# A root first on ScalarE, the last batch's gates and output tiles by halves of the sequence, and another order

## The chip, the cores and the metric

The kernel runs on one core of one Trainium2 chip. The core has five engines with their own instruction streams: TensorE (PE, matrix products into the PSUM banks), VectorE (DVE), ScalarE (ACT), GpSimd (POOL) and SyncE (SP, which here only issues DMAs). They wait for one another through semaphores. The metric is the device time of one execution in microseconds; three executions of the kernel before were timed, and one more was profiled.

## The reference

Two stages follow each other, for 4 batches, 8 heads, a sequence of 768 and heads of 64.

- Routed attention. Each query and each key is assigned to the one of 16 centroids of its head that it is most similar to: `argmax(q/|q| . c/|c|)`. A query attends only to the keys of its own cluster: `softmax(where(same cluster, q.k/8, -1e9)) @ v`.
- A gated long convolution. The attention output `x` (4 x 768 x 512) is projected, `x1, x2, x3 = split(x @ w_proj)`; `x2` is convolved along the sequence by FFT with `filter`; the output is `(x1 * irfft(rfft(x2) * rfft(filter)) * x3) @ w_out`, float32, 4 x 768 x 512.

## The kernel before, in words

Work is cut into 8 groups (`n`, two per batch: half of the heads each) of two head pairs (`pr`). Per pair and key tile `sk`, TensorE makes the scores in three banks, ScalarE takes the exponential (lines 694 and 697), TensorE multiplies by v into a PSUM pair (line 708), and VectorE adds up the row sums (lines 725 and 729). Cluster masks are rows added to the score product: the routing of group n+1 runs beside the attention of group n, ends with one-hot rows `ohT`, and small DMAs (line 497, "aug<-ohT") put them below the q and k operands `aug`. Group 0 has no attention to hide behind: its routing (`first_masks`) is the start of the kernel, together with the centroids' normalization (lines 336 to 361, with a root on ScalarE at line 342), the cosine and sine tables of the transform (`angles`, lines 364 to 409, whose `turns` on line 377 or 379 is the first step) and constants (`constants`, lines 1003 to 1070).

The convolution of batch b (`hyena`) runs beside later attention; for the last batch nothing is left beside it. It does the forward transform (line 843 and `spectrum4`), the product with the filter's spectrum (873, 877), and then, for each of four blocks `dt` of 128 channels: the gates `G` (line 903: products for x3 and x1 in two halves `ch` of the sequence, evacuated by lines 912 and 915 into `x3`), the inverse transform `I` (926), a copy of one bank (940), folds by sum and difference into `yy` (946; of the two folds the first writes the first half of the sequence), and the product with the gates into `y2` (955). Six output tiles of 128 positions then go through `W` (981): each contracts over the four blocks of `y2`. In the last batch a tile's product is split into its first three blocks and its fourth block (985 and 987), the sixth tile is made in two halves of its columns (967 to 977), and the first two tiles share one store of 512 KB (998), while tiles 2, 3, 4 are stored singly (994) and the sixth in two halves (975).

The order of all instructions on all engines is made by a planner in the file (`Plan.place`). Each operation has a cost per engine, a due time, and the operations it depends on; the planner takes, engine by engine, the ready operation with the earliest due time. `NUDGE` holds a correction to the due time for each operation, by its running number, and `ONLY` fixes the engine of some. `after=` adds a dependency that the planner alone sees: it orders, and makes no semaphore. ScalarE needs a table for its functions; `tab=` tells the planner of it, and a table is loaded by an instruction ACT_TABLE_LOAD.

In the lists of operations below, most products of the convolution and the scores have line 84, because the helper `product` records them; they are told apart by their tiles.

Of the kernel before, what the change touches and what calls it, by code (L numbers as in the profile page):

```python
# [264 lines left out]
def build(T):  # L265
# [25 lines left out]
    def bank(i):  # L291
        return T.bank[i][:]
# [71 lines left out]
    def angles(sq):  # L364
        sins = []
        MAGIC = 12582912.0
        sc = math.pi / S
        for m in range(3):
            lo = 256 * (m // 2)
            n, r = (lambda x=x, m=m, lo=lo: x()[m % 2][:, lo // 256, :384].rearrange("p (i c) -> p i c", i=2) for x in (lambda: T.tm, lambda: T.ob))  # L370
            nk, rk = ("tm", m % 2, "a", m), ("ob", m % 2, "a", m)
            kc = lambda: T.kc
            due = 1.9 + .8 * m
            V = lambda: T.nc.vector
            def turns(e, m=m, r=r):
                if e == "ACT":
                    T.nc.scalar.activation(r(), kc(), Act.Identity, scale=T.s1t[:, m:m + 1], bias=T.magic)
# [5 lines left out]
            op(("DVE", .56), lambda e, m=m, n=n, r=r: V().scalar_tensor_tensor(  # L383
                n(), kc(), T.s0t[:, m:m + 1], r(), op0=Alu.mult, op1=Alu.add), due + .2, r=["kc", "s0t", rk], w=[nk],
               lock=True)
            def mirror(e, n=n, r=r):
                if e == "ACT":
                    T.nc.scalar.activation(r(), n(), Act.Abs)
                else:
                    V().scalar_tensor_tensor(r(), n(), -1.0, n(), op0=Alu.mult, op1=Alu.max)  # L390
            op({"DVE": .56, "ACT": .55}, mirror, due + .3, r=[nk], w=[rk], lock=True)
            A_ = lambda: T.nc.scalar.activation
            sins.append(op(("ACT", .52), lambda e, m=m, n=n: A_()(cols_(T.fwm[m][:, 1]), n(), Act.Sin, scale=sc),
                           due + 6, r=[nk], w=[("fw", m, 1)], after=[sq], tab="sin"))
# [12 lines left out]
        sins.append(op(("ACT", .39), phases, 9.5, r=["kp", "half_pi"], w=["ph"], after=[sq], tab="sin"))  # L407
        return [op(("ACT", .2), lambda e: T.nc.scalar.activation(T.warm, T.half_pi, Act.Exp), 9.6, r=["half_pi"],
                   w=["warm"], after=sins, tab="exp")]
# [164 lines left out]
    def routing(n):  # L574
# [56 lines left out]
        for ch in range(2):  # L631
            op(("DVE", .6), lambda e, ch=ch, h=h: V().transpose(T.sim[:, ch], bank(h.ids[ch])[:, :384]), b0 + 1.4 + .1 * ch,
               r=[h], w=[("sim", ch, 0), ("sim", ch, 1)], free=[h])
# [183 lines left out]
    def hyena(b):  # L817
# [66 lines left out]
        for dt in range(ND):  # L884
# [13 lines left out]
            for ch in range(2):  # L898
                for off in (2 * DM, 0):
                    h = Bank()  # L900
                    due = step(.66)

                    def G(e, dt=dt, ch=ch, off=off, h=h):
                        for kt in range(ND):
                            x = T.xT[xs][:, kt, ts(ch, 384)].rearrange("p (t n) -> p t n", n=128)
                            columns(ap(h)[:, :384].rearrange("p (t n) -> p t n", n=128), T.wpj[:, kt, off + dt * 128:off + dt * 128 + 128],
                                    x[:, :, ::-1] if ch else x, kt == 0, kt == ND - 1)
                    g = op(("PE", .648), G, due, r=XT + WPJ, w=[h], alloc=h, kind="proj",
                           after=gs[-1:] + (inv[dt - 2:dt - 1] if dt > 1 else []))
                    gs.append(g)  # L910
                    if off:
                        op(EV384, lambda e, ch=ch, x3=x3, h=h: copy(e, x3()[:, ch], ap(h)[:, :384]), due + .8,
                           r=[h], w=xkeys[ch], free=[h])
                    else:
                        op(("DVE", .55), lambda e, ch=ch, x3=x3, h=h: T.nc.vector.tensor_tensor(
                            x3()[:, ch], ap(h)[:, :384], x3()[:, ch], op=Alu.mult), due + .8,
                           r=[h], w=xkeys[ch], free=[h])
# [23 lines left out]
            for s_, o_ in ((0, Alu.add), (1, Alu.subtract))[:0 if whole else 2]:  # L941
                op(("DVE", .55), lambda e, s_=s_, o_=o_, hh=hh, sd=sd, od=od: T.nc.vector.tensor_tensor(
                    sd()[:, s_].rearrange("p a b -> p (a b)"), bk(hh, 0)[:, :384], od(), op=o_), due + 1.5,
                   r=[hh] + okeys, w=skeys[s_::2], free=[hh])
            for s_, o_ in ((0, Alu.add), (1, Alu.subtract)):
                def fold(e, s_=s_, o_=o_, yy=yy, sd=sd, hh=hh, od=od, whole=whole):
                    o = yy().rearrange("p t (g q) -> p g t q", g=2)
                    if whole:
                        x = [y[:, :384].rearrange("p (g t q) -> p g t q", g=2, q=64) for y in (bk(hh, 0), od())]
                    else:  # L950
                        x = [sd()[:, :, k].rearrange("p g (t q) -> p g t q", q=64) for k in range(2)]
                    alu(e).tensor_tensor((o[:, ::-1, ::-1, ::-1] if s_ else o)[:, :, :3], x[0], x[1], op=o_)
                op(("DVE", .55) if whole else {"DVE": .55, "POOL": 1.2}, fold, due + 2, r=[hh] + okeys if whole else skeys, w=ykeys[s_::2], lock=not whole,
                   free=[hh] if whole else [])
            op(("DVE", .95) if last else {"DVE": .95, "POOL": 2.1}, lambda e, dt=dt, x3=x3, yy=yy: alu(e).tensor_tensor(  # L955
                T.y2[:, dt], yy().rearrange("p t c -> p (t c)"), x3().rearrange("p a b -> p (a b)"),
                op=Alu.mult), due + 2.5, r=ykeys + xkeys[0] + xkeys[1], w=[("y2", dt)], lock=True)
        for tt in range(3):
            ob, obk = (T_("tm", 0), [("tm", 0, 0), ("tm", 0, 1), ("tm", 0)]) if last and tt == 2 else (
                T_("ob", tt % 2), [("ob", tt % 2, 0), ("ob", tt % 2, 1), ("ob", tt % 2)])  # L960
            for e_ in range(2):
                due = step(.87)
                if last and tt == 2 and e_:
                    for x in range(2):
                        h, cols = Bank(), ts(x, DM // 2)

                        def half(e, kts, cols=cols, h=h):
                            for kt in kts:
                                columns(ap(h)[:, :DM // 2], T.y2[:, kt, ts(NT - 1, 128)], T.wout[:, kt, cols], kt == 0, kt == ND - 1)
                        op(("PE", .36), lambda e, half=half: half(e, range(3)), due, r=[("y2", dt) for dt in range(3)] + WOUT,  # L970
                           w=[h], alloc=h, kind="proj")
                        op(("PE", .12), lambda e, half=half: half(e, range(3, 4)), due, r=[("y2", 3), h], w=[h], kind="proj")
                        op({"ACT": .37, "DVE": .42}, lambda e, cols=cols, ob=ob, h=h: copy(e, ob()[:, 1, cols], ap(h)[:, :DM // 2]), due + 1,
                           r=[h], w=[("end", x)], free=[h])
                        op({"ACT": .4, "SP": .4}, lambda e, cols=cols, ob=ob: dma(e)(
                            T.out[b].rearrange("(p t) m -> p t m", t=NT)[:, NT - 1, cols], ob()[:, 1, cols]), due + 2,
# [298 lines left out]
```

## Time and profile before

| what | value |
|---|---|
| median of three executions | 375.29 us (373.97, 375.29, 375.74) |
| the profiled execution's own time | 374.39 us |
| its span, first to last instruction | 372.7 us |
| PE busy | 359.1 us (96%) |
| DVE busy | 344.9 us (93%) |
| ACT busy | 263.9 us (71%) |
| POOL busy | 116.3 us (31%) |
| granted clock of TensorE | 1.000 |

An engine is busy while it executes. The profile lists, beside each group of instructions, how long its engine had been idle just before it and what ended that idleness. The "chain that ended last" is followed back from the last instruction, at each step to what released it. A DMA is listed twice: its issue on an engine's queue, and the time from issue to landing. Lines marked PEld are loads of weights, which overlap products.

### The profile page before, as it was taken

Reading aid. Unit: us, or ns where it says so; the run is one execution under the profiler, and the core shown is the slowest. Engines: PE = TensorE matmul, PEld = TensorE weight load, DVE = VectorE, ACT = ScalarE, POOL = GpSimd, SP = SyncE. Lnnn points to the kernel's source line nnn. Section 1 sums busy time; section 2 is a strip of 40 time slices with the busy share of each in tenths; the row PEclk is TensorE's granted clock in tenths of the full one; section 3 lists DMA queues with packets and bytes.
Section 4 is the critical chain, followed back from the end, with each engine's and each line's share of the span. In section 5 each row is a group of like instructions: output and inputs, shape, how many; then the busy total and the mean of one; then the engine's idle time right before and its main releaser. Section 6 shows DMA issues by size and latency. Waiting matters only on the chain.

```text
span 372.7 us, 8638 instructions
## 1 busy us (share of the span) xinstructions
PE 359.1 (96%) x3322; PEld 207.4 (56%) x3322; DVE 344.9 (93%) x477; ACT 263.9 (71%) x497; POOL 116.3 (31%) x158
## 2 busy tenths in 40 slices
PE   7899999999999999999999999989999999999894
PEld 3556455555654565665555556657454556566571
DVE  6998999998999899999999999998997999999993
ACT  5999878788994758788769756689764759433332
POOL 5723151220113644223223136343211342033610
PEclk9999999999999999999999999999999999999999
DMA  7879469563478748678747957357655841111204
GB/s 161 206 152 187 97 151 240 121 131 107 79 169 163 113 78 161 114 162 124 170 56 143 216 161 150 74 73 98 167 57 135 187 109 13 44 45 58 108 9 169
DMA packets 90261, 46.20 MB, mean 124 GB/s; under 512 B 78232, under 2 KB 84076, under 8 KB 90220
## 3 DMA queue, kind: packets, MB, share of 16 engines
q1 hardware_dynamic: 85308, 35.59, 39.9%
q0 software_dynamic: 2752, 8.98, 17.6%
q10 hardware_dynamic: 2160, 1.08, 1.0%
q8 instruction: 26, 0.43, 0.5%
q14 instruction: 15, 0.12, 0.1%
HBM read 31.59 MB, written 7.40 MB: 105 GB/s over the span
## 4 chain that ended last, share of the span: by engine, by line
PE 66%; DVE 20%; issue 4%; DMA 4%; SPq 2%; ACT 2%; ACTq 0%; DVEq 0%
PE bank L84 29%; PE pair L708 26%; DVE acc L729 5%; PE bank L594 4%; PE bank L843 3%; DMA aug<-ohT 3%; PE bank L627 3%; DVE tm L873 2%; SPq L497 1%; DMA qkraw<-in_q_dram 1%; DVE qkP L284 1%; DVE aug L284 1%; SPq L323 1%; PE bank L742 1%; DVE xT L808 1%
## 5 line engine op out<-in xcount | busy, mean ns | idle before, releaser
L708 PE MATMUL pair<-p,vraw 128*64 128x385 f32 x768 | 142.5, 489 | 0.0
L697 ACT ACTIVATE p<-bank 128x512 f32<-128x512 f32 x192 | 109.4, 609 | 24.2 <-PE bank L84 18.1
L729 DVE TENSOR_TENSOR acc<-p,acc 128x1536 f32<-128x1536 f32 x64 | 112.8, 1763 | 4.4 <-POOL acc L725 1.5
L84 PE MATMUL bank<-aug,aug 80*64 80x512 bf16 (+3 forms) x742 | 80.6, 326 | 2.4 <-DMA aug<-ohT 0.9
L708 PEld LDWEIGHTS pair<-p,vraw 128*64 128x64 f32 x768 | 55.6, 136 | 45.4 <-issue 38.0
L84 PEld LDWEIGHTS <-aug 80*64 80x64 bf16 (+1 forms) x742 | 44.9, 109 | 39.4 <-issue 24.7
L694 ACT ACTIVATE p<-bank 128x512 f32<-128x512 f32 x96 | 58.1, 606 | 5.8 <-PE bank L84 4.3
L84 PE MATMUL bank<-xT,wpj 128*64 128x384 bf16 x512 | 48.0, 326 | 0.2 <-ACT ohT L653 0.2
L284 POOL CAST aug<-qkP 64x768 bf16<-64x768 f32 x27 | 23.5, 875 | 74.8 <-PE bank L84 33.6
L762 POOL DMA_DIRECT2D acc<-acc x30 | 24.0, 809 | 71.9 <-DMA acc<-acc 37.1
L84 PEld LDWEIGHTS <-wpj 128*64 128x64 bf16 x512 | 30.7, 110 | 15.0 <-issue 5.2
L282 ACT COPY qkP<-bank 128x512 f32<-128x512 f32 (+1 forms) x48 | 24.3, 550 | 14.5 <-PE bank L594 9.6
L84 PEld LDWEIGHTS <-y 128*64 128x64 bf16 x472 | 23.7, 110 | 14.5 <-issue 4.3
L725 POOL TENSOR_TENSOR acc<-p,p 128x512 f32<-128x512 f32 x15 | 19.1, 1277 | 37.0 <-DVE acc L725 13.9
L873 DVE TENSOR_TENSOR tm<-bank,hm 128x512 f32<-128x512 f32 x44 | 28.1, 682 | 1.7 <-PE bank L475 0.6
L877 POOL TENSOR_TENSOR y<-tm 128x512 bf16<-128x512 f32 x15 | 19.0, 1277 | 18.1 <-DVE tm L873 5.8
L84 PE MATMUL bank<-wout,y 128*64 128x512 bf16 (+1 forms) x200 | 23.3, 371 | 0.2 <-DVE y L955 0.2
L843 PE MATMUL bank<-wpj,xT 128*64 128x512 bf16 x192 | 22.5, 379 | 0.0
L725 DVE TENSOR_TENSOR acc<-p,p 128x512 f32<-128x512 f32 x33 | 21.8, 692 | 0.1
L594 PEld LDWEIGHTS bank<-ident,qkraw 128*128 128x128 f32 x144 | 15.6, 141 | 6.2 <-issue 3.3
L594 PE MATMUL bank<-ident,qkraw 128*128 128x128 f32 x144 | 18.4, 277 | 0.1
L282 ACT CAST aug<-qkP 64x768 bf16<-64x768 f32 x21 | 17.2, 828 | 1.0 <-DVE qkP L284 0.7
(179 smaller groups left out, 432.7 us busy)
## 6 DMA issues: line engine op xcount, KB each, us to landing
vraw<-in_v_dram SPq DMA_DIRECT2D x16, 384.0 KB, 4.3
qkraw<-in_k_dram SPq DMA_DIRECT2D x30, 192.0 KB, 3.3
rb<-dr SPq DMA_DIRECT2D x30, 192.0 KB, 3.7
qkraw<-in_q_dram SPq DMA_DIRECT2D x29, 192.0 KB, 4.2
out_dram<-ob SPq DMA_DIRECT2D x10, 512.0 KB, 3.9
acc<-acc POOLq DMA_DIRECT2D x10, 384.0 KB, 5.5
acc<-acc POOLq DMA_DIRECT2D x10, 192.0 KB, 4.2
y<-in_moe_filter_fft_dram SPq DMA_DIRECT2D x4, 384.0 KB, 6.2
```

What stands on the lines that cost most here:

```text
L84: T.nc.tensor.matmul(out[64 * i:64 * i + 64], lhsT[:, 64 * i:64 * i + 64], rhs, start=start, stop=stop)
L282: T.nc.scalar.copy(out, in_)
L284: (T.nc.vector if e == "DVE" else T.nc.gpsimd).tensor_copy(out, in_)
L594: T.nc.tensor.transpose(bank(h.ids[i // 4])[:, ts(i % 4, 128)], raw(ss[i // NT], i % NT), T.ident[:, ::-1] if 3 <= i < NT else T.ident)
L694: T.nc.scalar.activation(o, ap(h).rearrange("p (a b) -> p a b", a=2), Act.Exp, scale=0.125)
L697: T.nc.scalar.activation(flat(s)[:, lo:lo + 512], ap(h), Act.Exp, scale=0.125)
L708: T.nc.tensor.matmul(o[64 * hp:64 * hp + 64, ch, :385], T.vraw[vs][:, hp, sk * D:(sk + 1) * D], T.p[slots[sk]][:, hp, 384 * ch:384 * ch + ...
L725: alu(e).tensor_tensor(o, x, y, op=Alu.add)
L729: T.nc.vector.tensor_tensor(T.acc[os], T.p[slots[sk]][:, :, :S], T.acc[os], op=Alu.add)
L762: op(("POOL", .8), lambda e, rows=rows: T.nc.gpsimd.dma_start(flat_()[:rows], flat_()[rows:2 * rows], accum_op=Alu.add), te, r=[], w=AK, b ...
L843: T.nc.tensor.matmul(ap(h)[64 * i:64 * i + 64], T.xT[xs][:, kt, c:c + 64], T.wpj[:, kt, DM:2 * DM], start=kt == 0, stop=kt == ND - 1)
L873: op(("DVE", .68), lambda e, i=i, cs=cs, r=r, h=h: T.nc.vector.tensor_tensor(T.tm[r][:, cs], ap(h), hmrow(i, (0, 2, 2, 3)[2 * r + cs]), op ...
```

## The change

- **Root first.** The memset of `half_pi` is now the first of the constants, and the activation `warm` (a square root of that constant, which loads the table with the root) is kept in a list `root`. `turns` and the zeroing copies `zero` get `after=root`, so the planner places no ScalarE computation ahead of it. The plan's cost of `turns` on ScalarE becomes 0.7 instead of 0.55, that of `tri` 2.0 instead of 1.6, and that of the routing's transposes 0.57 instead of 0.6.
- **Halves.** In the last batch the gates get a due time of their own (all first halves ahead of the second halves), and they no longer wait in the plan for the gate before them and the inverse transform two blocks earlier. The product into `y2` is made in two halves of the sequence, and an output tile depends only on the half that it lies in. The first three tiles are one product over all four blocks; the fourth and fifth, and the halves of the sixth, are still split.
- **Single stores.** The first two tiles of the last batch are stored singly, like the others.
- **Order.** All corrections `NUDGE` (1,941 before, 1,943 now) and the list `ONLY` are other ones.

```diff
-NUDGE = {0:-134.893,1:-852.116,2:-3.912,3:-64.112,4:-7.409, ...
-ONLY = {14:"POOL",15:"POOL",17:"POOL",18:"POOL",29:"ACT", ...
+NUDGE = {0:-244.575,1:-2716.133,2:-17.613,3:-10.463,4:-13.793,5:-22.114, ...
+ONLY = {13:"POOL",14:"POOL",15:"POOL",16:"POOL",18:"POOL",30:"ACT", ...
...
-            op({"DVE": .36, "ACT": .55, "POOL": .95}, turns, due, r=["kc", "s1t", "magic"], w=[rk], lock=True)
+            op({"DVE": .36, "ACT": .7, "POOL": .95}, turns, due, r=["kc", "s1t", "magic"], w=[rk], lock=True, after=root)
...
                 for off in (2 * DM, 0):
                     h = Bank()
                     due = step(.66)
+                    if last:
+                        due = w1 - 8 + 5 * ch + dt
...
                     g = op(("PE", .648), G, due, r=XT + WPJ, w=[h], alloc=h, kind="proj",
-                           after=gs[-1:] + (inv[dt - 2:dt - 1] if dt > 1 else []))
+                           after=[] if last else gs[-1:] + (inv[dt - 2:dt - 1] if dt > 1 else []))
...
-            op(("DVE", .95) if last else {"DVE": .95, "POOL": 2.1}, lambda e, dt=dt, x3=x3, yy=yy: alu(e).tensor_tensor(
-                T.y2[:, dt], yy().rearrange("p t c -> p (t c)"), x3().rearrange("p a b -> p (a b)"),
-                op=Alu.mult), due + 2.5, r=ykeys + xkeys[0] + xkeys[1], w=[("y2", dt)], lock=True)
+            for ch in range(2) if last else [slice(0, 2)]:
+                cols = slice(384 * ch, 384 * ch + 384) if last else slice(0, S)
+                op(("DVE", .55) if last else {"DVE": .95, "POOL": 2.1}, lambda e, dt=dt, ch=ch, cols=cols, x3=x3, yy=yy: alu(e).tensor_tensor(
+                    T.y2[:, dt, cols], yy().rearrange("p t c -> p (t c)")[:, cols],
+                    x3()[:, ch] if last else x3().rearrange("p a b -> p (a b)"), op=Alu.mult), due + 2.5,
+                   r=ykeys[ch::2] + xkeys[ch] if last else ykeys + xkeys[0] + xkeys[1],
+                   w=[("y2", dt, ch)] if last else [("y2", dt, 0), ("y2", dt, 1)], lock=True)
+        Y2 = lambda tile, dts: [("y2", dt, tile // 3) for dt in dts]
...
-                if last:
-                    op(("PE", .647), lambda e, W=W: W(e, range(3)), due, r=[("y2", dt) for dt in range(3)] + WOUT,
+                if last and 2 * tt + e_ > 2:
+                    op(("PE", .647), lambda e, W=W: W(e, range(3)), due, r=Y2(2 * tt + e_, range(3)) + WOUT,
                        w=[h], alloc=h, kind="proj")
-                    op(("PE", .217), lambda e, W=W: W(e, range(3, 4)), due, r=[("y2", 3), h], w=[h], kind="proj")
+                    op(("PE", .217), lambda e, W=W: W(e, range(3, 4)), due, r=Y2(2 * tt + e_, [3]) + [h], w=[h], kind="proj")
                 else:
-                    op(("PE", .862), W, due, r=[("y2", dt) for dt in range(ND)] + WOUT, w=[h], alloc=h,
+                    op(("PE", .862), W, due, r=Y2(2 * tt + e_, range(ND)) + WOUT, w=[h], alloc=h,
                        kind="proj")
...
-                if last and tt and not (tt == 2 and e_):
+                if last and not (tt == 2 and e_):
                     op({"SP": .4, "ACT": .4}, lambda e, tt=tt, e_=e_, ob=ob: dma(e)(
                         T.out[b].rearrange("(p t) m -> p t m", t=NT)[:, 2 * tt + e_], ob()[:, e_]), due + 2,
                        r=[obk[e_]], byts=157e3)
-            if not (last and tt):
+            if not last:
                 op(("SP", .4), lambda e, tt=tt, ob=ob: T.nc.sync.dma_start(
...
+    root = []
+
     def constants():
         G = lambda: T.nc.gpsimd
+        op(("POOL", .1), lambda e: G().memset(T.half_pi, math.pi / 2), -1, w=["half_pi"])
...
-        op(("POOL", .1), lambda e: G().memset(T.half_pi, math.pi / 2), -1, w=["half_pi"])
-        op(("ACT", .2), lambda e: T.nc.scalar.activation(T.warm, T.half_pi, Act.Sqrt), -1, r=["half_pi"], w=["warm"], tab="sqrt")
+        root.append(op(("ACT", .2), lambda e: T.nc.scalar.activation(T.warm, T.half_pi, Act.Sqrt), -1, r=["half_pi"], w=["warm"], tab="sqrt"))
...
-                op({"POOL": .8, "ACT": .83}, zero, 3 + (1, 1, 28)[i] * i, r=["ident"], w=[("zero", i, j)], lock=True)
+                op({"POOL": .8, "ACT": .83}, zero, 3 + (1, 1, 28)[i] * i, r=["ident"], w=[("zero", i, j)], lock=True, after=root)
```

More of the change, by code (lines that the diff above doesn't have):

```diff
@@ L43 @@
-ONLY = {14:"POOL",15:"POOL",17:"POOL",18:"POOL",29:"ACT",32:"SP",33:"SP",36:"SP",37:"ACT",39:"SP",40:"SP",41:"DVE",47:"ACT",67:"POOL",71:"ACT",85:"ACT",86:"DVE",88:"DVE",89:"DVE",91:"DVE",94:"ACT",97:"DVE",99:"ACT",100:"DVE",101:"POOL",139:"ACT",141:"DVE",143:"ACT",147:"DVE",149:"DVE",159:"ACT",176:"POOL",226:"POOL",227:"POOL",232:"POOL",233:"ACT",239:"POOL",244:"POOL",245:"DVE",253:"DVE",254:"DVE",256:"ACT",257:"ACT",357:"POOL",359:"POOL",394:"ACT",405:"DVE",407:"POOL",408:"ACT",409:"POOL",410:"ACT",412:"DVE",413:"DVE",415:"ACT",418:"DVE",426:"ACT",461:"DVE",462:"POOL",463:"DVE",498:"DVE",508:"ACT",513:"ACT",523:"POOL",533:"POOL",541:"DVE",551:"DVE",555:"ACT",559:"DVE",562:"DVE",570:"ACT",600:"DVE",608:"POOL",616:"ACT",640:"DVE",688:"ACT",690:"ACT",691:"ACT",692:"DVE",693:"DVE",694:"ACT",697:"ACT",700:"DVE",701:"POOL",702:"POOL",808:"DVE",809:"DVE",860:"POOL",861:"POOL",862:"POOL",867:"POOL",913:"POOL",914:"POOL",986:"DVE",1024:"DVE",1054:"ACT",1067:"ACT",1070:"ACT",1072:"ACT",1094:"DVE",1145:"POOL",1147:"POOL",1153:"POOL",1155:"POOL",1164:"DVE",1165:"ACT",1168:"DVE",1313:"POOL",1314:"POOL",1315:"DVE",1368:"DVE",1416:"DVE",1500:"DVE",1515:"POOL",1547:"DVE",1549:"POOL",1600:"ACT",1601:"ACT",1607:"POOL",1608:"POOL",1621:"DVE",1767:"DVE",1874:"DVE",1940:"SP"}
@@ new lines @@
+ONLY = {13:"POOL",14:"POOL",15:"POOL",16:"POOL",18:"POOL",30:"ACT",32:"SP",33:"SP",36:"SP",37:"SP",40:"ACT",41:"DVE",66:"ACT",69:"DVE",72:"POOL",73:"ACT",85:"DVE",86:"DVE",93:"DVE",94:"POOL",97:"DVE",99:"DVE",100:"DVE",101:"POOL",141:"DVE",153:"DVE",213:"ACT",226:"POOL",227:"POOL",233:"POOL",238:"POOL",244:"POOL",245:"DVE",253:"DVE",254:"ACT",257:"DVE",288:"DVE",357:"POOL",358:"DVE",359:"POOL",394:"ACT",404:"ACT",406:"DVE",407:"DVE",408:"POOL",409:"ACT",416:"POOL",417:"POOL",418:"POOL",427:"DVE",430:"ACT",461:"POOL",462:"DVE",463:"DVE",498:"DVE",525:"POOL",533:"POOL",549:"DVE",551:"ACT",555:"ACT",566:"DVE",589:"DVE",593:"POOL",594:"POOL",600:"DVE",604:"DVE",639:"DVE",691:"POOL",692:"ACT",693:"POOL",694:"POOL",696:"ACT",697:"ACT",698:"ACT",699:"POOL",700:"POOL",701:"DVE",711:"DVE",808:"POOL",809:"POOL",856:"DVE",858:"ACT",859:"ACT",861:"POOL",862:"POOL",867:"POOL",913:"DVE",915:"POOL",1002:"DVE",1005:"DVE",1018:"DVE",1067:"ACT",1070:"DVE",1072:"ACT",1075:"ACT",1077:"DVE",1146:"POOL",1147:"POOL",1152:"DVE",1153:"DVE",1154:"POOL",1156:"ACT",1164:"ACT",1168:"ACT",1201:"DVE",1313:"DVE",1315:"ACT",1369:"DVE",1416:"ACT",1421:"ACT",1426:"ACT",1448:"DVE",1457:"DVE",1516:"POOL",1600:"POOL",1601:"POOL",1607:"POOL",1608:"POOL",1609:"POOL",1610:"DVE",1621:"DVE",1812:"ACT",1875:"DVE",1886:"DVE",1919:"ACT",1920:"SP",1922:"DVE",1923:"SP",1926:"SP",1930:"SP",1933:"ACT",1934:"SP",1938:"SP",1942:"SP"}
@@ L631, in routing @@
         for ch in range(2):
-            op(("DVE", .6), lambda e, ch=ch, h=h: V().transpose(T.sim[:, ch], bank(h.ids[ch])[:, :384]), b0 + 1.4 + .1 * ch,
+            op(("DVE", .57), lambda e, ch=ch, h=h: V().transpose(T.sim[:, ch], bank(h.ids[ch])[:, :384]), b0 + 1.4 + .1 * ch,
                r=[h], w=[("sim", ch, 0), ("sim", ch, 1)], free=[h])
@@ L969, in half @@
                                 columns(ap(h)[:, :DM // 2], T.y2[:, kt, ts(NT - 1, 128)], T.wout[:, kt, cols], kt == 0, kt == ND - 1)
-                        op(("PE", .36), lambda e, half=half: half(e, range(3)), due, r=[("y2", dt) for dt in range(3)] + WOUT,
+                        op(("PE", .36), lambda e, half=half: half(e, range(3)), due, r=Y2(2 * tt + e_, range(3)) + WOUT,
                            w=[h], alloc=h, kind="proj")
-                        op(("PE", .12), lambda e, half=half: half(e, range(3, 4)), due, r=[("y2", 3), h], w=[h], kind="proj")
+                        op(("PE", .12), lambda e, half=half: half(e, range(3, 4)), due, r=Y2(2 * tt + e_, [3]) + [h], w=[h], kind="proj")
                         op({"ACT": .37, "DVE": .42}, lambda e, cols=cols, ob=ob, h=h: copy(e, ob()[:, 1, cols], ap(h)[:, :DM // 2]), due + 1,
@@ L1044, in tri @@
             G().tensor_tensor(T.tri[:].rearrange("p (b c) -> p b c", c=NC), x, T.ident[:].rearrange("p (b c) -> p b c", c=NC), op=Alu.subtract)
-        op(("POOL", 1.6), tri, 14, r=["ident"], w=["tri", ("rb", 0), ("rb", 1)])
+        op(("POOL", 2.0), tri, 14, r=["ident"], w=["tri", ("rb", 0), ("rb", 1)])
         def first_(e):
```

2 lines of the change are left out of this document (1 added, 1 removed).

## The prediction

> **What bounds the kernel now.** I read the page's table of engines first, then the busy time by stages, then the chain that ended last at both ends of the span. The rows of the stages give, for each engine, the busy time within the stretch:
>
> ```profile
> span 372.7 us, 8638 instructions
> PE 359.1 (96%) x3322; PEld 207.4 (56%) x3322; DVE 344.9 (93%) x477; ACT 263.9 (71%) x497; POOL 116.3 (31%) x158
> ...
> 10.00:25.00 15.00, 13.32 (x126) 8.34 (x126) 14.06 (x33) 14.38 (x30) 8.83 (x19) 1.00 0.89 191
> 25.00:330.00 305.00, 302.38 (x2739) 171.70 (x2738) 288.27 (x365) 229.67 (x433) 88.84 (x93) 1.00 0.63 126
> 330.00:367.50 37.50, 36.08 (x437) 23.74 (x435) 35.05 (x63) 13.62 (x27) 12.94 (x10) 1.00 0.13 51
> ```
>
> From 25 to 330 us PE is busy for 302.38 of 305.00 us: the body is TensorE's, and no order can take more than 2.62 us out of it. From 10 to 25 the full engines are ACT (14.38 of 15) and DVE (14.06), and PE stands still for 1.68. From 330 to 367.5 PE (36.08 of 37.5) and DVE (35.05) share the bound, and ACT has two thirds of the time free. After 367.5 only copies and stores are left. So the change can win at the two ends, and its new order can win little and lose much between them.
>
> **The start.** ScalarE's own sequence, in order of time:
>
> ```profile
> 1.82 1.28 ACT L377 ACT_TABLE_LOAD   x1 [1.82 <-DVE s1t L1029]
> 3.12 1.30 ACT L377 ACTIVATE ob<-x,magic,s1t 128x384 f32<-128x384 f32 x2
> 4.33 0.83 ACT L1060 ACTIVATE aug<-ident 64x768 bf16<-64x768 f32 x1
> ...
> 7.12 0.84 ACT L1060 ACTIVATE aug<-ident 64x768 bf16<-64x768 f32 x1 [1.97 <-DMA qkraw<-in_q_dram]
> 7.98 1.28 ACT L342 ACT_TABLE_LOAD   x1
> ...
> 9.28 0.20 ACT L342 ACTIVATE s<-ss 128x1 f32<-128x1 f32 x1
> 9.39 0.84 ACT L282 COPY qkP<-bank 128x384 f32<-128x384 f32 x2
> ...
> 10.34 1.28 ACT L393 ACT_TABLE_LOAD   x1
> ...
> 18.99 1.28 ACT L408 ACT_TABLE_LOAD   x1
> ```
>
> There are four table loads in the span: these two, one ahead of the sines at 10.34 and one ahead of the first exponential at 18.99. The first load serves `turns`, which isn't a root; after the root's load at 7.98 a copy runs at 9.39 with no further load. With the root first, its table serves turns, zeros and copies, and the load at 7.98 goes: -1.28 us of ACT. The other two stay.
>
> Is it on the path? VectorE's rows say how much:
>
> ```profile
> 8.12 0.15 DVE L341 TENSOR_SCALAR ss<-ss 128x1 f32<-128x1 f32 x1
> 8.20 0.61 DVE L383 SCALAR_TENSOR_TENSOR tm<-x,s0t,ob 128x384 f32<-128x384 f32 x1
> 8.84 0.56 DVE L390 SCALAR_TENSOR_TENSOR ob<-tm 128x384 f32<-128x384 f32 x1
> ```
>
> The root's input is there at 8.27, so the root could run 1.0 us earlier; but DVE fills that second with lines 383 and 390, work that must be done anyway. Hence only the relief of ACT counts, in a stretch where both ACT and DVE are full and several copies can go to either. `ONLY` also pins five of the six zeros to POOL where it pinned four, which takes one more zero (0.84 us, the row at 7.12) from ACT. POOL pays 0.74 us for it, and has 6.2 us free between 10 and 25:
>
> ```profile
> L1058 POOL MEMSET aug<- 64x768 bf16 x4 | 2.9, 744 | 3.1 <-DVE ob L390 3.0
> ```
>
> Together ACT loses 1.28 + 0.84 = 2.1 us; spread over two full engines that is about 1.0 us. Since the loads of q and k end part of the waits, I take **-0.7 us**. Ends: -1.68 (all of PE's standstill) and +0.2: the root itself, 0.20 us, now stands between the first load and `turns`, whose result DVE needs.
>
> The moved memset takes 0.10 us on POOL; by its due time it passes the iotas and the identity on POOL's queue, which feed `s1t` and DVE's first turn. I cost it at nothing: its cover is the 1.82 us that ACT stands idle ahead of its first load. Without that cover it is 0.10. On ACT's queue the root passes two turns, two zeros and a copy pair; those wait for 0.20 us more. The other changed planner costs move no work by themselves.
>
> **The end.** First the chain that ended last, then TensorE's list and the copies and issues behind it:
>
> ```profile
> 361.94 0.56 DVE qkP L915
> 362.50 0.46 DVE sim L952
> 362.96 0.46 DVE qkP L915
> 363.42 0.47 DVE sim L952
> ...
> 363.92 0.97 DVE y L955
> ```
>
> ```profile
> 352.56 1.43 PE L84 MATMUL bank<-inv,y 128*64 128x192 bf16 x30 [1.12 <-DVE y L877]
> ...
> 361.66 3.08 PE L84 MATMUL bank<-wout,y 128*64 128x512 bf16 x30
> 364.93 2.46 PE L84 MATMUL bank<-wout,y 128*64 128x256 bf16 x26 [0.19 <-DVE y L955]
> ```
>
> ```profile
> 367.22 0.37 ACT L282 COPY tm<-bank 128x256 f32<-128x256 f32 x1
> ...
> 367.44 0.69 DVE L284 COPY ob<-bank 128x512 f32<-128x512 f32 x1 [0.61 <-PE bank L84]
> ...
> 367.63 0.36 ACTq L975 DMA_DIRECT2D out_dram<-tm  x1
> 368.16 0.47 ACTq L994 DMA_DIRECT2D out_dram<-ob  x1
> ```
>
> ```profile
> L994 ACTq DMA_DIRECT2D out_dram<-ob x2: 374/420/466, 366.2 to 368.2; - x2
> ...
> DMA to landing us min/median/max: 3.2/3.2/3.2
> ```
>
> ```profile
> L975 ACTq DMA_DIRECT2D out_dram<-tm x1: 362/362/362, 367.6 to 367.6; - x1
> ...
> DMA to landing us min/median/max: 3.0/3.0/3.0
> ```
>
> Call T the end of the last product into `y2`, 363.92 + 0.96 = 364.88. All six tiles wait for it. Behind it: 26 products, 2.46 us, to 367.41; a copy to 368.13; an issue at 368.16, landed 3.2 us later, at 371.4 (the row of line 994); and 1.3 us to the end of the span.
>
> After the change only tiles 3 and 4 and both halves of tile 5 need T, each for its fourth block. The 26 products are 16 wide and 10 half-wide ones, 21 wide equivalents at 0.117 us; 4 wide and 4 half-wide are left behind T, 6 equivalents, **0.70 us** instead of 2.46. Last then is a half tile: copy 0.37, issue 0.03 later, landing in 3.0 (what the half tile's store on line 975 took), and the same 1.3: T + 0.05 + 0.70 + 0.02 + 0.37 + 0.03 + 3.0 + 1.34 = T + 5.5, where it was T + 7.8. The single stores of tiles 0 and 1 are one issue more and come earlier, beside other work; if not, an issue costs 0.36 to 0.47 us (the rows above).
>
> But T moves. The 1.76 us of products go ahead of T, where PE's only idle time from 351 on is 1.12 + 0.19 = 1.31 us. The gates, freed from the gate and the inverse ahead of them, are what could fill the 1.12 (`xT`, which they read, is written long before, and in this batch each block has its own `x3`), so T is pushed by at least 0.45. VectorE pays too: `y2` in halves costs two operations less their overlap. The chain's row pairs a 128x384 operation of 0.56 with a next one that adds 0.46, so a pair is 1.02 against 0.95; four pairs, +0.28. T later by 0.45 + 0.28 = 0.73 us gives an end at T(before) + 6.2, **-1.6 us**. Ends: -2.3 (T unmoved) and +0.6 (nothing earlier, and no overlap in the halves: 2 x 0.56 - 0.97 = 0.15, four times).
>
> [...]
>
> **The body.** All corrections of the order are new, and the diff doesn't tell where each instruction lands. The rows nearest to it are the three waits of PE around one handover of masks from one group to the next:
>
> ```profile
> 242.88 0.84 PE L84 MATMUL bank<-xT,wpj 128*64 128x384 bf16 x8 [0.21 <-ACT ohT L653]
> ...
> 248.90 0.52 PE L84 MATMUL bank<-aug,aug 128*64 128x256 bf16 x4 [0.94 <-DMA aug<-ohT]
> ...
> 249.89 0.90 PE L84 MATMUL bank<-aug,aug 80*64 80x512 bf16 x6 [0.47 <-ACT p L694]
> ```
>
> Together they are 1.62 us of the body's 2.62. I take **0**: the same products by the same engine. Ends: -2.6 (none of it left) and +4.9 (three more handovers of the seven like this one).
>
> **Sum.** -0.7 - 1.6 + 0 = -2.3 us. Against the profiled execution's 374.39 that is 372.1; that execution lies 0.9 under the median of the three timed. I put the sum to the mean of all four, 374.85: **372.6 us**. A difference of 0.5%, 1.9 us, is about what this kernel's measurement can tell from none.
>
> **Rivals.**
>
> *The end stays as it is* (374.1). The last stores are bound by bandwidth, not by T:
>
> ```profile
> 366.80:367.80 1.00, 0.60 (x8) 0.12 (x4) 0.39 (x2) 0.79 (x2) 0.00 (x0) 1.00 0.80 299
> ...
> 369.80:370.80 1.00, 0.00 (x0) 0.00 (x0) 0.00 (x0) 0.00 (x0) 0.00 (x0) 1.00 1.01 370
> ```
>
> For these four slices the DMA share is 0.8 to 1.07 at 299 to 406 GB/s, which moves the last batch's 1.57 MB. If PE, full until T, finishes tiles 0 to 2 only just before T, their stores still queue with the others, and the end gains nothing: -0.7 alone, 374.1. Against it: the first half's last product into `y2` needs only the fold at 362.50, and at its 0.56 us could end near 363.9.
>
> *Slower: late masks in the body* (377.4). The new order puts the mask chain of more groups too late, and PE, which has no slack there, waits at each handover for the DMA "aug<-ohT", then for an exponential, as at 248.90. Price 1.62 each. Two eat the gain (2.3 / 1.62 = 1.4); from three on the kernel is slower by over 0.5%: 374.85 - 2.3 + 4.9 = 377.4. For it: PE is at 99% there, so any slip shows. Against it: before, one handover in seven did so.
>
> *The body gains too* (370.0): -2.3 - 2.6. Against it: every wait would have to go, though the new order was free to move them.
>
> *The first computation isn't the root's or its load isn't saved*: -1.6 alone, 373.2, still inside the forecast's own spread.
>
> **How the numbers follow.** Forecast with its spread (371.7 to 374.1: for the start -1.2 to -0.25 and for the end -1.95 to -0.5, half way to the bounds of each): 0.50, of which 0.10 within 0.5% of no change. End unchanged: 0.16, nearly all within. Late masks: 0.26, of which 0.03 within. Body gains: 0.08, faster. That makes faster 0.40 + 0.08 + 0.02 = 0.50, same 0.10 + 0.14 + 0.03 = 0.27, slower 0.23. The range reaches from 370.0, the case in which the body gains, to 378.0, past three late handovers; about one in ten lies beyond each end.
>
> **What would show it.** Three table loads, the first ahead of line 1050's activation, and none at the centroids' root; the first exponential 0.7 us earlier. At the end: products into `y2` as eight 128x384 ones of 0.55; at most 0.8 us of tile products behind the last of them; stores starting more than 1.5 us ahead of the last; 5.5 us from T to the end of the span. In the body: PE's idle time between 25 and 330 us near 2.6. The prediction is wrong if that idle time is above 5, if T comes more than 1.5 us later against the end of attention, or if PE waits for the first group's routing longer than before.

## The result, and the profile after

The changed kernel takes **370.86 us** (370.64 to 371.05, four executions), the kernel before 375.48 (373.97 to 375.74): a ratio of 0.9885, with a 95% interval of 0.9858 to 0.9912. The forecast was 372.6. The profiled executions differ by less: 370.64 against 374.39, spans 368.9 against 372.7, so 3.8 us of the 4.6 can be looked for in the traces.

First the head of the page of the changed kernel and its busy time by stages (columns as in the prediction: stretch, its length, then busy time and instructions of PE, PEld, DVE, ACT, POOL, the granted clock, the DMA share, GB/s):

```profile
span 368.9 us, 8653 instructions
PE 357.5 (97%) x3314; PEld 208.9 (57%) x3316; DVE 342.5 (93%) x478; ACT 263.6 (71%) x495; POOL 120.9 (33%) x162
10.00:25.00 15.00, 13.92 (x128) 7.79 (x130) 14.20 (x28) 13.74 (x29) 9.17 (x28) 1.00 0.88 190
25.00:330.00 305.00, 302.55 (x2745) 175.41 (x2745) 287.85 (x367) 230.11 (x431) 91.59 (x93) 1.00 0.61 126
330.00:364.70 34.70, 33.55 (x412) 21.68 (x408) 32.45 (x62) 12.37 (x25) 12.96 (x10) 1.00 0.17 65
```

PE stands idle for 2.45 us of the body, against 2.62. So the body is still TensorE's, and the gain is at the ends. Five moments make that exact: the first and the last product of attention (line 708), T (the end of the last product into `y2`), the first store's issue, and the end of the span.

| us | first product | last product ends | T | first store | end |
|---|---|---|---|---|---|
| before | 26.48 | 325.90 | 364.88 | 365.68 | 372.7 |
| after | 24.77 | 322.58 | 362.43 | 361.83 | 368.9 |

The start is 1.71 shorter, attention 299.42 → 297.81 (-1.61), and what follows it 46.8 → 46.3 (-0.5). The middle one is mostly no gain. The busy time of the instructions that read or write `xT`, the operand of the projection, says where it went. Each fence has two rows, attention and what follows it; the columns are the stretch, its length, PE, PEld, DVE, the granted clock, the DMA share and GB/s. First before, then after:

```profile
25.00:325.90 300.90, 49.70 (x492) 8.50 (x144) 14.63 (x14) 1.00 0.63 127
325.90:367.40 41.50, 20.25 (x216) 2.75 (x48) 2.24 (x3) 1.00 0.15 55
```

```profile
25.00:322.58 297.58, 48.19 (x470) 8.76 (x144) 14.09 (x14) 1.00 0.63 128
322.58:364.63 42.05, 21.67 (x232) 2.90 (x48) 2.15 (x3) 1.00 0.17 63
```

Sixteen gate products, 1.42 us of PE, have moved behind the last product of attention. For equal work, that is with these 1.42 us counted where they were, the body is 0.2 shorter and the end 1.9.

ScalarE and VectorE in the start of the changed kernel, in order of time:

```profile
1.27 1.31 ACTq L323 DMA_DIRECT2D qkraw<-in_k_dram  x2
2.62 1.28 ACT L1059 ACT_TABLE_LOAD   x1 [2.62 <-issue]
3.92 0.20 ACT L1059 ACTIVATE warm<-half_pi 128x1 f32<-128x1 f32 x1
...
5.36 0.51 ACT L388 ACTIVATE ob<-tm 128x384 f32<-128x384 f32 x1
5.77 0.19 ACT L342 ACTIVATE s<-ss 128x1 f32<-128x1 f32 x1
...
6.46 0.51 ACT L388 ACTIVATE ob<-tm 128x384 f32<-128x384 f32 x1
6.99 1.28 ACT L395 ACT_TABLE_LOAD   x1
...
21.02 1.28 ACT L408 ACT_TABLE_LOAD   x1
...
22.93 0.60 ACT L697 ACTIVATE p<-bank 128x512 f32<-128x512 f32 x1 [0.41 <-PE bank L84]
```

```profile
8.22 1.02 DVE L284 COPY qkP<-bank 128x384 f32<-128x384 f32 x2
...
14.06 0.55 DVE L529 TENSOR_REDUCE mx<-bank 128x24 f32<-128x384 f32 x1
```

The last of these rows, in the kernel before:

```profile
16.61 0.56 DVE L529 TENSOR_REDUCE mx<-bank 128x24 f32<-128x384 f32 x1
```

There are three table loads of 1.28 us, and the centroids' root at 5.77 has none ahead of it: between the loads at 2.62 and 6.99 ScalarE runs the root of the constant, turns, a zero, mirrors and the centroids' root. Two mirrors of the angles (`Abs`, line 388) run on ScalarE where VectorE had all three (line 390), ScalarE issues two loads ahead of its table, and the one-hot steps (line 529) begin at 14.06, where they began at 16.61.

The end of the changed kernel: TensorE, then VectorE, then SyncE.

```profile
357.87 0.28 PE L84 MATMUL bank<-wout,y 128*64 128x256 bf16 x2
359.22 5.41 PE L84 MATMUL bank<-wout,y 128*64 128x256 bf16 x54 [1.07 <-DVE y L959]
```

```profile
354.88 1.02 DVE L959 TENSOR_TENSOR y<-yy,qkP 128x384 bf16<-128x384 f32 x2
...
361.88 0.55 DVE L959 TENSOR_TENSOR y<-sim,qkP 128x384 bf16<-128x384 f32 x1
...
364.67 0.69 DVE L284 COPY ob<-bank 128x512 f32<-128x512 f32 x1 [1.90 <-PE bank L84]
```

```profile
361.83 0.33 SPq L982 DMA_DIRECT2D out_dram<-tm  x1
...
363.55 2.17 SPq L1001 DMA_DIRECT2D out_dram<-ob  x4
```

And the first store before:

```profile
365.68 0.33 SPq L975 DMA_DIRECT2D out_dram<-tm  x1
```

The tile products run without a gap from 359.22 to 364.63, 2.2 us beyond T (361.88 + 0.55 = 362.43). The last is a whole tile of the **first** half of the sequence (512 wide, copied at 364.67); the tiles of the second half went ahead.

### The profile page after: what moved, and what is told of

It reads as the page before. It is cut to its first block, busy times and chain, and to the rows that moved or that the text cites. A ratio compares the mean times of both kernels' runs of the same rounds, so it can differ in the third digit from the quotient of the medians.

```text
span 368.9 us, 8653 instructions
## 1 busy us (share of the span) xinstructions
PE 357.5 (97%) x3314; PEld 208.9 (57%) x3316; DVE 342.5 (93%) x478; ACT 263.6 (71%) x495; POOL 120.9 (33%) x162
## 4 chain that ended last, share of the span: by engine, by line
PE 78%; DVE 11%; ACT 5%; issue 3%; DMA 1%; POOL 1%; SPq 0%; DVEq 0%; ACTq 0%; POOLq 0%
PE bank L84 33%; PE pair L708 28%; PE bank L843 5%; PE bank L594 5%; DVE acc L729 3%; PE bank L627 2%; ACT p L697 1%; PE bank L82 1%; DMA qkraw<-in_k_dram 1%; DVE qkP L284 1%; PE bank L475 1%; PE bank L742 1%; ACT p L694 1%; PE bank L607 1%; DVE ohT L655 1%
## 5 line engine op out<-in xcount | busy, mean ns | idle before, releaser
L84 PE MATMUL bank<-aug,aug 80*64 80x512 bf16 (+3 forms) x736 | 81.9, 327 | 2.1 <-ACT p L697 0.9
L708 PEld LDWEIGHTS pair<-p,vraw 128*64 128x64 f32 x768 | 56.6, 136 | 43.8 <-issue 36.7
L284 POOL CAST aug<-qkP 64x768 bf16<-64x768 f32 x29 | 25.9, 900 | 83.3 <-DVE acc L729 55.9
L84 PE MATMUL bank<-xT,wpj 128*64 128x384 bf16 x504 | 47.2, 326 | 0.0
L282 ACT COPY qkP<-bank 128x512 f32<-128x512 f32 (+1 forms) x46 | 23.1, 559 | 15.9 <-PE bank L594 9.7
L282 ACT CAST aug<-qkP 64x768 bf16<-64x768 f32 x28 | 23.2, 830 | 1.0 <-DVE qkP L284 0.4
L877 POOL TENSOR_TENSOR y<-tm 128x512 bf16<-128x512 f32 x14 | 17.8, 1277 | 12.8 <-DVE tm L873 10.6
L732 ACT COPY osb<-pair 128x770 f32<-128x770 f32 x16 | 12.9, 806 | 10.8 <-PE pair L708 10.7
```

Of the source, the lines that this page charges most:

```text
L84: T.nc.tensor.matmul(out[64 * i:64 * i + 64], lhsT[:, 64 * i:64 * i + 64], rhs, start=start, stop=stop)
L282: T.nc.scalar.copy(out, in_)
L284: (T.nc.vector if e == "DVE" else T.nc.gpsimd).tensor_copy(out, in_)
L708: T.nc.tensor.matmul(o[64 * hp:64 * hp + 64, ch, :385], T.vraw[vs][:, hp, sk * D:(sk + 1) * D], T.p[slots[sk]][:, hp, 384 * ch:384 * ch + ...
```

## The experiments

The two theories at the outset: **P**, the parts (root first, halves, single stores) bring the gain; **O**, the new order brings it, whatever the parts. The gates' own due times, and their freedom from the gate and the inverse transform ahead of them, count as order here: e2, e3 and e4 keep them, e6 and e7 don't have them. All moments are those of the table above, idle time is PE's between 25 us and the last product of attention. Ratios are to the kernel before, run beside them on the same chip.

| run | first product | last product | T | first store | end | idle | ratio [95%] |
|---|---|---|---|---|---|---|---|
| before | 26.48 | 325.90 | 364.88 | 365.68 | 372.7 | 2.62 | |
| after | 24.77 | 322.58 | 362.43 | 361.83 | 368.9 | 2.45 | 0.9885 [0.9858, 0.9912] |
| e1 after, root late | 25.63 | 323.35 | 363.19 | 362.59 | 369.7 | 2.30 | 0.9920 [0.9893, 0.9947] |
| e2 after, whole products | 25.08 | 322.90 | 363.19 | 364.30 | 371.1 | 2.21 | 0.9949 [0.9913, 0.9985] |
| e3 after, paired store | 24.88 | 322.63 | 362.48 | 361.87 | 369.4 | 2.29 | 0.9890 [0.9840, 0.9941] |
| e4 order alone | 25.64 | 324.83 | 365.13 | 366.24 | 373.4 | 3.73 | 0.9971 [0.9935, 1.0007] |
| e5 before, root first | 26.20 | 325.86 | 364.84 | 365.63 | 372.6 | 2.86 | 0.9956 [0.9919, 0.9993] |
| e6 before, halves | 26.51 | 327.33 | 366.85 | 366.80 | 374.2 | 4.16 | 0.9989 [0.9954, 1.0025] |
| e7 before, all parts | 26.18 | 328.29 | 367.79 | 367.74 | 375.1 | 4.53 | 0.9979 [0.9949, 1.0010] |
| e8 after, copies spread | 25.07 | 322.71 | 362.55 | 361.95 | 369.0 | 2.19 | 0.9875 [0.9832, 0.9919] |
| e9 before, root and mirrors | 26.24 | 325.51 | 364.16 | 364.95 | 371.9 | 2.32 | 0.9973 [0.9938, 1.0008] |
| e10 after, mirrors on DVE | 25.60 | 322.96 | 362.82 | 362.21 | 369.3 | 2.17 | 0.9898 [0.9857, 0.9938] |
| e11 after, casts on DVE | 26.87 | 324.55 | 364.39 | 363.78 | 370.9 | 2.38 | 0.9924 [0.9894, 0.9953] |
| e12 e9 and one load earlier | 25.36 | 325.79 | 364.41 | 365.20 | 372.2 | 3.63 | 0.9934 [0.9898, 0.9969] |

### Parts taken out of the changed kernel

In the edits, `move(n, m)` puts operation n right behind m in the finished order, or first where m is None.

**e1**, the root behind the centroids' root again:

```diff
     order = P.place(...)
+    move(10, 25)    # 10: warm; 25: the centroids' root
```

> The changed kernel with its own order, but the root of the constant moved on ScalarE from first place to behind the centroids' root; nothing else moves. Theory P (the parts bring the gain: at the start the saved table load): a load of 1.28 us returns ahead of the centroids' root, the first product with v comes 1.0 to 1.3 us later than in the changed kernel (24.77 us), and the time is 371.9 to 372.1 us. Theory O (the new order brings it, whatever the parts): the first product with v comes at most 0.3 us later, 370.9 to 371.1 us.

The first product comes 0.86 later, less than the 1.0 to 1.3 expected, and the end of the span 0.8; the median is 372.17 us. In this order the root is worth 0.86 of its load's 1.28 us, and ScalarE has four table loads again.

**e2**, the product into `y2` whole, and all tiles split 3 + 1 as before; every other operation keeps its correction of the due time:

```diff
-            for ch in range(2) if last else [slice(0, 2)]:
...
+            op(("DVE", .95) if last else {"DVE": .95, "POOL": 2.1}, lambda e, dt=dt, x3=x3, yy=yy: alu(e).tensor_tensor(
+                T.y2[:, dt], yy().rearrange("p t c -> p (t c)"), x3().rearrange("p a b -> p (a b)"), op=Alu.mult), due + 2.5,
+               r=ykeys + xkeys[0] + xkeys[1], w=[("y2", dt, 0), ("y2", dt, 1)], lock=True)
...
-                if last and 2 * tt + e_ > 2:
+                if last:
```

> The changed kernel, but in the last batch the product with the gates into y2 in one piece per block, and tiles 0 to 2 split in three blocks and one as before; the order is the same up to these operations, and the planner places them anew. Theory P: every tile waits for the last product into y2, the time from its end to the end of the span grows from 6.5 us to 7.5 or more, and the time is 371.9 to 372.5 us. Theory O (TensorE has no time free ahead of that product, so it only changes which tiles come first): within 0.4 us of the changed kernel, 370.5 to 371.3 us.

373.47 us, 2.6 above the changed kernel and above the range expected by P; the spans differ by 2.2. From the last product of attention to the end it is 48.2 us, 1.9 more than 46.3. TensorE's list shows the price, a gap:

```profile
358.18 0.38 PE L84 MATMUL bank<-wout,y 128*64 128x512 bf16 x2
361.12 1.92 PE L84 MATMUL bank<-wout,y 128*64 128x512 bf16 x16 [2.56 <-DVE y L961]
363.24 3.44 PE L84 MATMUL bank<-wout,y 128*64 128x512 bf16 x38 [0.20 <-DVE y L961]
```

**e3**, tiles 0 and 1 in one store of 512 KB again:

```diff
-                if last and not (tt == 2 and e_):
+                if last and tt and not (tt == 2 and e_):
...
-            if not last:
+            if not (last and tt):
```

> The changed kernel, but tiles 0 and 1 of the last batch in one store of 512 KB. Theory P: the pair waits for the later of the two copies and moves twice the bytes at the end, 0.2 to 0.5 us more, 371.1 to 371.4 us. Theory O: no difference above 0.2 us.

371.2 us, and 0.5 more of span. One slice of the last transfers shows why; the slices beside it have 0.97 and more:

```profile
364.40:365.40 1.00, 0.27 (x4) 0.00 (x0) 0.69 (x1) 0.14 (x1) 0.00 (x0) 1.00 1.02 382
365.40:366.40 1.00, 0.00 (x0) 0.00 (x0) 0.00 (x1) 0.00 (x0) 0.00 (x0) 1.00 0.55 213
366.40:367.40 1.00, 0.00 (x0) 0.00 (x0) 0.00 (x0) 0.00 (x0) 0.00 (x0) 1.00 0.97 401
```

The store waits for the second of its tiles (the copy ends at 365.40, the issue is at 365.46), and the DMA engines run half empty meanwhile (0.55).

**e4**, the three edits together, so that of the change only the order is left:

> The changed kernel's order with all three parts undone (root late, products into y2 whole, pair store). Theory P: the sum of the three losses, 1.1 + 1.3 + 0.3, 373.3 to 374.0 us, so that the order alone gives about 2 us of the 4.6. Theory O: at most 1 us of loss, 370.9 to 371.9 us.

374.18 us, a ratio whose interval reaches 1. The order alone gives 0.84 of the start. From the last product to the end it is 48.6 us against 46.8; 1.42 of that are the moved gates, and the gap of e2 stands in it, so that for equal work the end is 0.4 longer. The 1.9 of e2 and the 0.5 of e3 make up the 2.3 by which this end is longer than the changed kernel's 46.3. Theory O falls in its simple form.

### Parts put into the kernel before

**e5** (first edit), **e6** (second edit: the product into `y2`, its dependents and the stores as in the change's diff; the first three tiles stay split 3 + 1) and **e7** (both), in the old order:

```diff
     order = P.place(...)
+    move(9, None)    # half_pi's memset
+    move(10, 30)     # warm, behind ScalarE's first load of q
```

```diff
+            for ch in range(2) if last else [slice(0, 2)]:
...
-                if last and tt and not (tt == 2 and e_):
+                if last and not (tt == 2 and e_):
```

> The kernel before with its own order; only the memset of the constant moves to the front of GpSimd's queue and the root of it to the front of ScalarE's computations. Theory P: one table load fewer, the first product with v 0.4 to 0.7 us earlier than at 26.48 us, 374.6 to 375.0 us. Theory O: the load goes, but VectorE has other work in that second, so the first product with v moves by less than 0.3 us, 375.2 to 375.6 us.

> The kernel before with its own order up to the last batch's products into y2; these are made in halves, each output tile depends on its half, and tiles 0 and 1 are stored singly; the gates keep their order. Theory P: the end gains 1.0 to 1.6 us, 373.9 to 374.5 us. Theory O (PE is full until the last product into y2, so nothing can be taken ahead of it): at most 0.4 us, 375.1 to 375.5 us.

> Both of the former: the kernel before with its own order, the root first, the halves and the single stores. Theory P: the sum of the two, 373.2 to 373.8 us. Theory O: 374.9 to 375.5 us.

The root alone moves the first product by 0.28 us (ratio 0.9956); the halves alone give 376.71 us, a ratio of 0.9989; all parts 0.9979. From the last product to the end it is 46.9 in e6 and 46.8 in e7, where it was 46.8. So P falls too: **in the old order the parts bring nothing that can be told (0.9979), in the new one 0.9% or 3.3 us (e4 to after, 0.9971 to 0.9885, 374.18 to 370.86 us)**. Each needs the other. For the halves the reason is in e2 and e6: the new order puts nearly all tile products behind the gates, where whole products into `y2` leave PE waiting for 2.56 and 0.20 us, and halves cut that to the one wait of 1.07 in the list of the changed kernel. The old order has no such gap to fill: in the prediction's rows PE waits there for 1.12 and 0.19, in e6 for 1.1 and 0.5.

**e8** swaps two of the last copies between VectorE and ScalarE in the changed kernel, to have the last copy on the free engine:

```diff
+ONLY.update({1929: "DVE", 1922: "ACT"})
```

The expectation counts the tiles from one: operation 1929 copies tile 3 in the numbering from zero that is used above, and 1922 copies tile 1, the last one.

> The changed kernel with the last copies of output tiles spread differently: the copy of tile 4 moves from ScalarE to VectorE, which stands idle there for 1.9 us, and the last one, of tile 2, from VectorE to ScalarE. The last copy is then 0.59 instead of 0.69 us and the stores ahead of it leave up to 0.5 us earlier: 0.1 to 0.4 us less, 370.4 to 370.8 us. If the end is set by the last tile's product alone, 0.1 us less at most.

371.96 us (370.81 to 373.38), span 369.0: no difference that can be told. The stores of this run:

```profile
361.95 0.33 SPq L983 DMA_DIRECT2D out_dram<-tm  x1
...
363.67 2.06 SPq L1002 DMA_DIRECT2D out_dram<-ob  x4
```

Counted from the first store, the last issue ends at 3.78 us instead of 3.89, as was meant, but the span ends at 7.1 in both. Three slices of the changed kernel fit that, with the DMA engines full (0.98 to 1.02):

```profile
363.90:364.90 1.00, 0.73 (x8) 0.14 (x4) 0.23 (x1) 0.60 (x2) 0.00 (x0) 1.00 0.98 352
364.90:365.90 1.00, 0.00 (x0) 0.00 (x0) 0.46 (x1) 0.00 (x0) 0.00 (x0) 1.00 1.02 383
365.90:366.90 1.00, 0.00 (x0) 0.00 (x0) 0.00 (x0) 0.00 (x0) 0.00 (x0) 1.00 0.98 385
```

So within this 0.1 us the last tile doesn't set the end. That the stores' volume does, counted from the first issue, is argued from the full engines.

### What else shortens the start

The root's 0.86 leaves half of the 1.71 open.

**e9**, in the kernel before, root first and two mirrors on ScalarE; **e10**, the changed kernel with these back on VectorE; **e11**, the changed kernel with three casts on VectorE:

```diff
+    move(9, None)
+    move(10, 30)
+    for n in (44, 56):
+        find(n).on = "ACT"
```

```diff
+    for o in order:
+        if o.seq in (44, 56):
+            o.on = "DVE"
```

For e11 the last has (66, 73, 95) in place of (44, 56).

> The kernel before with the root first, as in the run with the root alone, and two of the three mirrors of the first features (the operation of line 390) on ScalarE, where the changed order has them. Theory V (VectorE's queue up to its last one-hot step sets the start, so what is taken off it comes back): 2 x 0.56 us leave VectorE, ScalarE does them in 2 x 0.51, and the first product of attention comes about 1.0 us earlier than with the root alone, near 25.2 us; the body may take some of it back. Theory S (the start is set by ScalarE or by the loads): first product of attention within 0.3 us of the 26.2 us with the root alone, or later.

> The changed kernel with the same two mirrors back on VectorE, 2 x 0.56 us there, and 2 x 0.51 off ScalarE; nothing else moves. Theory V: first product of attention 0.9 to 1.1 us later than the 24.77 of the changed kernel, and the time later by about as much. Theory S: first product of attention and time within 0.3 us of the changed kernel's, since VectorE stands idle somewhere in that stretch.

> The changed kernel with three casts into aug (64x768), which its order gives to ScalarE (0.83 us each), back on VectorE (0.55 us each), where the kernel before has them. Theory V: up to 3 x 0.55 = 1.65 us more on VectorE ahead of the last one-hot step, so the first product of attention comes 1.0 to 1.7 us later than 24.77. Theory S: ScalarE gets 2.5 us free, and the first product of attention comes no later than in the changed kernel.

In the changed order VectorE's queue does set the start: e10 has the first product 0.83 later (0.9 to 1.1 were expected), e11 2.10 later (1.0 to 1.7 were expected), although ScalarE is busy for 0.9 and 4.2 us less between 10 and 25. Of e10's 0.83 only 0.4 is left at the end of the span. In the old order e9 gives nothing: 26.24 against 26.20. Its rows on TensorE and VectorE say why:

```profile
9.90 0.55 PE L607 MATMUL bank<-ident,qkraw 128*128 128x128 f32 x3 [2.33 <-DMA qkraw<-in_q_dram]
```

```profile
10.48 1.95 DVE L284 COPY qkP<-bank 128x384 f32<-128x384 f32 x4 [0.93 <-PE bank L607]
```

Most of the second that came free is spent waiting for transposes, and they wait until 9.90 for a load of q that ScalarE issues late.

**e12** adds that load early, behind ScalarE's first one (the changed order has it early too, on SyncE at 1.84):

```diff
+    move(37, 30)     # a half of q, 6.45 before
```

> The kernel before with the root first and two mirrors on ScalarE, as in the run before, and one more thing of the changed order: the load of a half of q that ScalarE issued at 6.45 us is issued behind its first load of q, near 1.9, ahead of the activations. In the run without this, VectorE stood idle for 0.93 us until 10.48, behind transposes that waited until 9.90 for that load. Theory V with loads (the relief of VectorE counts once the loads come early enough): transposes near 7.5, that idle time gone, and the first product of attention up to 0.9 us earlier than the 26.24 without it, 25.3 to 25.8. Theory B (the DMA engines are full in that stretch, so an earlier load makes another one late): the first product of attention within 0.3 us of 26.24, and the wait stands at another load.

25.36, 0.88 earlier than e9: the wait was the cover. (373.54 us, ratio 0.9934.) The load without the mirrors wasn't run; in e5 VectorE comes to these copies at 10.45 without a wait, so there was none for an earlier load to remove. The body gave the start back in this execution, by a wait of PE's:

```profile
65.04 1.51 PE L594 MATMUL bank<-ident,qkraw 128*128 128x128 f32 x12 [1.64 <-DMA qkraw<-in_q_dram]
```

### DMA waits in the body

That wait isn't e12's own. In the lists of PE's waits between 25 us and the end of attention, all six profiled kernels with the old order wait for the DMA "aug<-ohT", 0.5 to 1.0 us, and four of them (e5, e6, e7, e12) for a load into `qkraw` or `vraw` besides, 0.7 to 1.7. Of the eight with the new order none waits for a DMA there; e4's idle time of 3.73 has a wait of 1.4 for a row sum in it instead. The times fit in part: on one chip the kernel before took 373.66 to 378.45 us in 25 executions, e3 370.98 to 371.56 in 4, and e1 371.38 to 373.46 in 10; but e2 took 372.55 to 375.06 and e4 373.89 to 376.76 in 10 each, without such a wait in their profiles. Each kernel has one profile, so that these waits make the spread is argued and not shown.

The granted clock of TensorE is a second candidate. Of those 25 executions the six with a clock of 0.993 or less took 376.51 to 378.45 us, the eleven with 0.998 or more 373.66 to 377.87: it goes with a part of the spread and leaves most of it. It doesn't carry the verdict on the old order: by the medians of the executions at 0.997 or more alone, e4, e6 and e7 stand at 0.9986, 1.0002 and 1.0003 of the kernel before.

## Why the prediction was right, and where it wasn't

Faster, as forecast, and by more: -4.6 us instead of -2.3 (from the run's own medians), -3.8 in the traces. The 370.86 us lie inside the range, but below the forecast's own spread (371.7 to 374.1) and next to the 370.0 of the rival in which the body gains too. The traces show no such gain, so that closeness is chance.

**The start: mechanism half right, size wrong.** The saved load, the three loads in all, and their places were as predicted. The term was -0.7 and measured -1.71, just beyond its far end of -1.68. The step that failed is "DVE fills that second with lines 383 and 390, work that must be done anyway. Hence only the relief of ACT counts". In the old order it holds: the root alone gives 0.28 (e5). The new order moved work from VectorE to the relieved ScalarE, so VectorE gained the second too: two of the mirrors (line 390), worth 0.83 (e10), and three casts, worth 2.10 (e11). These don't add up to the whole, for other moves of the order cost some of it: without the root the order gives 0.84 in all (e4), and the root 0.86 on top (e1). The discount of 0.3 us for the loads of q and k was wrong too: such a wait is real (e9), but the order also moved the load (e12). "The first exponential 0.7 earlier" was 1.6: 24.53 to 22.93. A cost of the 0.20 us of the root on ScalarE's queue doesn't show; the first table load comes 0.8 later than before, behind two issues.

**The body: 0 was right for what was profiled** (-0.2, idle 2.45; the wait for "aug<-ohT" is gone and one of 0.7 for `ohT` is there instead). Neither the late masks nor a body that gains show in the trace. The 0.9 us by which the medians gain more than the profiles may come from the DMA waits or the granted clock above; that stays open.

**The end: size right by luck, path wrong.** Predicted -1.6, measured -1.9 for equal work. Two errors offset each other: T came 1.3 us earlier than forecast, and the stretch behind it is 1.0 longer.
- "0.70 us of products behind T" failed: it is 2.2. The step assumed that the first half's tiles go ahead; the order takes the second half's first, since both wait in line behind the gates. So "last is a half tile" and "T + 5.5" fell too: T + 6.5, where it was T + 7.8.
- T was to come 0.73 later against the end of attention: 39.85 against 38.98, +0.87. But 1.42 of that is the moved gates; without them it is earlier by 0.55.
- The price of a half was right: a single product is 0.55 us (361.88 above) and a pair 1.02 (354.88), as the fold's pair suggested.
- The single stores were costed at nothing. They gain 0.5 of span (e3): without them a transfer waits for its second tile.
- The rival "bound by bandwidth" had the path right, though not that the end stays as it is. From the first store's issue to the end are 7.0 us before and 7.1 after, 6.8 to 7.2 in the runs whose last transfers have no hole, 7.4 to 7.6 in the three with one (e3, e6, e7). Yet the end did gain, because the first store is issued 0.6 us before T instead of 0.8 after. This shift of 1.4 gives the 1.3 by which the stretch behind T is shorter; the products behind T gave only 0.3 (2.2, where it was 2.5). That the stores' volume sets the end rests on these times and on the 0.1 us of e8; no run changed the volume, and an order that takes the first half's tiles ahead of T wasn't run. "Stores starting 1.5 us ahead of the last" was no test: before they did already, by 2.5.

**What the prediction didn't see** is that terms of a change and of its order aren't additive here: it added the root, the halves and the order as separate terms, which is right only in the new order.

## What to carry to other kernels

Before crediting a saving on one engine, ask whether the schedule can move work from the full engine beside it into the freed time, and then which load that work waits for: here one freed table load was worth 0.28 us alone, and 1.7 together with the work and the loads that the order moved. An edit and the order of instructions that goes with it are tested together and apart (two by two), since each alone can measure as nothing. At a tail of stores look at when the first is issued and whether the DMA engines have a hole behind it, not only at the last: here a first issue 1.4 us earlier against T went with 1.3 us less behind T, and one hole with 0.5 us of span (e3).

## What wasn't expected

- The same parts in the old order made nothing that can be told (ratio 0.9979, to 1.0010), in the new one 0.9%.
- Two 128x384 products in a row on VectorE take 1.02 us where one takes 0.55: 0.08 of the second hides behind the first.
- The kernel before varies by 1.3% in 25 executions on one chip (373.66 to 378.45) and by 0.5% in the four of the result, the changed one by 0.1% in its four, e1, e2 and e4 by 0.6 to 0.8% in ten each; waits on DMAs in the body stand in all six profiles of the old order and in none of the eight of the new.
